# Value products joined with the next unit's scores, more early weight slots, and the gate's denominator sum on GpSimd for 24 steps

## The chip, the cores and the metric

The kernel runs on one core of one Trainium2 chip. The metric is the time of one execution in device microseconds; the runs shown of the kernel before took 986.03 to 987.42 us, with a median of 987.19 us. A separate execution was recorded by the profiler; everything said of single instructions comes from it. The engines are named as the profile names them: PE (TensorE's matmuls), PEld (its weight loads), DVE (VectorE), ACT (ScalarE), POOL (GpSimd), SP (SyncE, which issues the DMAs here).

## The reference

Sliding-window attention is followed by a feed-forward layer whose activation is a rational function.

```python
# q, k, v: (8, 8, 576, 64)
scores = q @ k.T / sqrt(64);  mask: 0 <= pos_q - pos_k < 64
attn = exp(scores - max);  attn = attn / (sum(attn) + 1e-9)
x = (attn @ v)  ->  (4608, 512)
h = x @ w_in                                  # w_in (512, 2048)
P = a[0] + a[1]*h + a[2]*h*h + a[3]*h*h*h
Q = 1 + |b[0]|*|h| + |b[1]|*h*h
g = P / (Q + 1e-6)
out = g @ w_out                               # w_out (2048, 512)
```

All inputs and the output are float32. The kernel keeps the two large products near float32 accuracy by splitting x, g and both weights into a high part (fp32r) and a low part and adding three products: low x high, high x high, high x low.

## The kernel before

**Tiling.** The 4608 tokens are cut into 12 chunks of 384. For each chunk the attention is computed in four *units*, one for each pair of heads, and the feed-forward layer in 16 *steps*, one for each 128 columns of the hidden layer. A unit is: score products (24 small matmuls into the PSUM tile `ps_s`, each on a 64x64 corner of the array), mask and maximum on DVE, exponentials with their sums on ACT, the division on DVE, six transposes on PE back into `ps_s`, a copy to `pT` on ACT, value products (24 matmuls of 128 rows by 64 columns into `ps_x`), and the split of the result into `xh` (ACT) and `xl` (DVE). A step is `ffn1` (12 matmuls of 384 columns into one of two `h` banks, then the gate) and, three steps later, `ffn2` (9 matmuls of 512 columns that add into the three `o` banks).

**The gate.** ACT makes u = h*h, r = |b0 h| and num = a3 h + a2. DVE adds u = |b1| u + r, the sum under the fraction without its constant. ACT takes the logarithm of u + 1.000001 and the exponential of its negative, which is the reciprocal r. DVE then makes the numerator in two operations on `num` (these read h from PSUM), and in four more, all on SBUF, the high part `gh`, and the low part `gl` with one correction. `r`, `u` and `num` have two buffers each, `gh` and `gl` four.

**Weights.** The 32 weight tiles (16 of w_in, 16 of w_out, 512 KB each) are fetched into three slots (`w_st`) and split by `load_weight`: a cast on ACT (`top`), a bit merge on DVE (`w_c`), a cast to the high part on ACT, a subtraction on DVE for the low part. A slot's next fetch is issued once its tile has been split. The first eight of each kind are loaded during the first eight steps, the others during the steps after them, so chunks 0 and 1 run their first eight steps, then chunk 1 and chunk 0 their last eight. Steps 0 to 23 are thus the ones beside which weights are split. The second half of the weights lives in tiles that share memory with the early q, k and v tiles (`early`) of chunk 0.

**What sets the order.** The kernel is recorded, not issued: each call on `pl` becomes an operation with a cost, and `plan` puts the operations of each engine in order by a small model of ready times, due order and costs. `group` makes several matmuls one piece that nothing is put between. Unit work of chunk c is recorded in the steps of the chunk that runs before it, at places given by `OFF` and `AHEAD`. In gaps of PE before the first `o` product, `fill` puts matmuls on a constant tile (`warm`). All instructions that are recorded carry the line of the recorder (L221, and L227 in the changed kernel), so the profile tells them apart by their tiles.

Of the kernel before, what the change touches and what calls it, by code (L numbers as in the profile page):

```python
# [9 lines left out]
F32 = mybir.dt.float32  # L10
# [22 lines left out]
OFF = dict(scores=0, soft=0, norm=0, transpose=1, av=1)  # L33
# [16 lines left out]
class Planner:  # L50
# [27 lines left out]
    @contextmanager  # L78
    def group(self, extra=0):
        g = self.group_op = Op()  # L80
# [24 lines left out]
    def cost(self, engine, method, out, reads, kw, args):  # L105
        if isinstance(out, Late):
            n = out.size // 4
        else:
            n = 1
            for _, k in out.ap[1:]:  # L110
                n *= k
        if engine == "SP":
            parts = 128 if isinstance(out, Late) else (out.ap[0][1] if out.tensor.__class__.__name__ != "DRamTensorHandle" else 0)
            size = mybir.dt.size(out.dtype) * n * (parts or out.ap[0][1])
            return 400, 400, size
        if engine == "PE":
            if method == "transpose":
                return 109, 270, 0
            if isinstance(args[2], Late):
                n = args[2].size // 4  # L120
            else:
                n = 1
                for _, k in args[2].ap[1:]:
                    n *= k
                if args[2].dtype == F32:
                    return (54, 270, 0) if args[1].ap[0][1] == 64 else (58, 225, 0)
            return n * 0.452, n * 0.452 + 165, 0
        if engine == "ACT":
            if "accum_out" in kw:
                return 343, 450, 0  # L130
            f = args[2] if len(args) > 2 else None
            occ = 58 + 0.813 * n
            if n == 512:
                occ = 640 if method == "copy" and getattr(out, "dtype", None) == F16 else 510
            for k in ("scale", "bias"):
                if isinstance(kw.get(k), bass.AP):
                    occ += 92
            if f in (AF.Ln, AF.Exp):
                occ += 55
            return occ, occ + 120, 0  # L140
        if engine == "DVE":
            if method == "tensor_reduce":
                n = 1
                for _, k in reads[0].ap[1:]:
                    n *= k
            if n < 16:
                return 90, 185, 0
            occ = 65 + 1.045 * n
            if isinstance(kw.get("scalar"), bass.AP):
                occ += 62  # L150
            return occ, occ + 85, 0
        if engine == "POOL":
            return (n * 2.0 + 60, n * 2.0 + 100, 0) if method == "tensor_scalar" else (n * 2.4 + 130, n * 2.4 + 170, 0)
# [24 lines left out]
    def plan(self):  # L178
# [6 lines left out]
        for _ in self.ops:  # L185
# [7 lines left out]
            if engine == "SP":  # L193
                dma_free = max(dma_free, start + 1500) + op.dma / 390
                op.end = dma_free + 150
# [47 lines left out]
def swa_rational_ffn(ctx: ExitStack, tc: tile.TileContext, qk, v, w_in, w_out, ab, out):  # L243
# [89 lines left out]
    UNIT = QK + TC * P  # L333
    qk_ring = Ring(ring, 2, [P, QK], F32, "qk")
# [12 lines left out]
    shares = {early[k].tensor.name: f"late_{n}" for k, n in enumerate(("wo_l", "wo_h"))}  # L347
# [7 lines left out]
    def fetch():  # L355
        if not fetch_order:
            return
        which, i = key = fetch_order.pop(0)
        staged[key] = w_ring()
        pl.sync.dma_start(out=staged[key].bitcast(U16)[:, 1:2049], in_=(w_in if which == "in" else w_out)[i])  # L360

    def load_weight(which, i):
# [10 lines left out]
        fetch()  # L373
# [6 lines left out]
    def load_qk(c, hp):  # L380
        qk_t = early[hp // 2][:, hp % 2 * UNIT:hp % 2 * UNIT + QK] if c == 0 else qk_ring()
# [3 lines left out]
        u["k"] = qk_t[:, CH:QK]  # L385

    def load_v(c, hp):
        vt = early[hp // 2][:, hp % 2 * UNIT + QK:hp % 2 * UNIT + UNIT] if c == 0 else vt_ring()
        live[c, hp]["vt"] = vt = vt.rearrange("p (t s) -> p t s", s=P)
        pl.sync.dma_start(out=vt, in_=v[hp, :, c * TC:(c + 1) * TC, :])  # L390
# [15 lines left out]
    def unit_scores(c, hp):  # L406
# [10 lines left out]
        with pl.group(340):  # L417
            for p in range(PR):
                for z in range(2):
                    for e in range(2):  # L420
                        j = 2 * p + e
                        pl.tensor.matmul(ps[z][e * 64:e * 64 + 64, p * P:(p + 1) * P], u["q"][z * 64:z * 64 + 64, j, :],
                                         u["k"][z * 64:z * 64 + 64, j * WIN:j * WIN + P], start=not on_pe, stop=not on_pe or p == PR - 1)
        sm, nmx = u["sm"], u["nmx"] = sm_ring(), small["nmx"]().rearrange("p (z r) -> p z r", z=2)
# [44 lines left out]
    def unit_av(c, hp):  # L469
        u = live.pop((c, hp))  # L470
        ps = ps_x[:, 0:TC * WIN].rearrange("p (t s) -> p t s", s=WIN)
        with pl.group(135):
            for j in range(TC):
                for z in range(2):
                    pl.tensor.matmul(ps[z * 64:z * 64 + 64, j, :], u["vt"][:, j, z * 64:z * 64 + 64],
                                     u["pT"][:, z, j * WIN:(j + 1) * WIN], start=True, stop=True)
        x = ps_x[:, 0:CH]
        xh, xl = (x_sb[x_slot(c)][part][hp] for part in range(2))
        pl.scalar.copy(out=xh, in_=x)
        pl.vector.tensor_tensor(out=xl, in0=x, in1=xh.bitcast(F32), op=ALU.subtract)  # L480

    gs = {}

    def ffn1(c, i):
        h = h_ring()[:, 0:CH]
        n = 0
        for cc in range(NCC):
            with pl.group():
                for w, x in (("wi_h", 1), ("wi_h", 0), ("wi_l", 0)):
                    pl.tensor.matmul(h, weight_piece(w, i, cc), x_sb[x_slot(c)][x][cc], start=n == 0, stop=n == 3 * NCC - 1)  # L490
                    n += 1
# [5 lines left out]
        pl.vector.scalar_tensor_tensor(out=u, in0=u, scalar=b_sb[:, 1:2], in1=r, op0=ALU.mult, op1=ALU.add)  # L497
# [66 lines left out]
    s, seen = 0, {0}  # L564
    for c, i0, i1 in phases:
        if c not in seen:
            seen.add(c)
            for k in range(HP):
                p = C1AT[k] if c == 1 else s - prev + prev // HP * k - AHEAD
                at(p, unit_load, c, k)  # L570
                for n, fn in (("scores", unit_scores), ("soft", unit_soft), ("norm", unit_norm), ("transpose", unit_transpose), ("av", unit_av)):
                    at(max(p + OFF[n], s - prev) if n == "av" else p + OFF[n], fn, c, k)
        prev = i1 - i0
        s += prev

    for load in (load_qk, 0), (load_qk, 1), fetch, (load_v, 0), (load_qk, 2), (load_v, 1), (load_qk, 3), fetch, (load_v, 2), (load_v, 3), None, fetch:
        if load is None:
            pl.sync.dma_start(out=ab_sb, in_=bass.AP(ab.tensor, 0, [[0, P], [1, 6]]))
        elif load is fetch:
            fetch()  # L580
        else:
            load[0](0, load[1])
# [6 lines left out]
    pl.scalar.activation(b_sb, b_raw, AF.Abs)  # L589
# [54 lines left out]
```

## Time and profile before

| | |
|---|---|
| median of the runs shown | 987.19 us |
| the profiled execution | 985.98 us |
| its span, first to last instruction | 984.2 us |
| PE busy | 959.3 us (97%) |
| DVE busy | 914.5 us (93%) |
| ACT busy | 693.1 us (70%) |
| POOL busy | 4.3 us, 20 instructions, all at the start |
| granted PE clock | 0.995 |

A row of a group or of the timeline names engine, operation, and then out<-in by the names of tiles, with the partitions and columns of each. In the timeline the first number is the start from the span's beginning, the second the duration; "x24" means that many records in a row, and a bracket behind a row tells how long the engine had stood still and what released it. Durations of neighbouring rows on one engine overlap by some 0.05 to 0.2 us, so what an instruction takes of its engine is read from start to start.

### The profile page before, as it was taken

What the parts mean: (1) busy time and instruction counts of PE and PEld (TensorE: products, weight loads), DVE (VectorE), ACT (ScalarE), POOL (GpSimd) and SP (SyncE); (2) the same over time, 40 slices, a digit from 0 to 9 for tenths busy, and PEclk for the clock granted to TensorE, in tenths of its full rate; (3) what the DMA queues carried; (4) which work ended last, traced back from release to release, by engine and by line L of the source; (5) the groups of instructions that cost most, each with busy time, mean ns of one, the idle gap of its engine ahead of it and who ended that gap; (6) DMA issues with size and microseconds to landing.
All of it is one profiled execution on the core that took longest, in us unless ns stands there. A gap on an engine that the chain in (4) does not pass through costs nothing.

```text
span 984.2 us, 17685 instructions
## 1 busy us (share of the span) xinstructions
PE 959.3 (97%) x6679; PEld 827.2 (84%) x6679; DVE 914.5 (93%) x1746; ACT 693.1 (70%) x1737; POOL 4.3 (0%) x20
## 2 busy tenths in 40 slices
PE   7798999999999999999999999999999999999998
PEld 4577788888888888888888888888888888888996
DVE  6899999899999999999999999999999999999997
ACT  6888877776667667666767677667666776766664
POOL 1000000000000000000000000000000000000000
PEclk9999999999999999999999999999999999999999
DMA  6654440313103103103102101210310310200000
GB/s 241 213 179 149 140 149 30 108 46 129 39 1 117 51 1 117 35 17 118 34 17 101 51 17 46 88 34 8 113 48 1 117 39 12 100 1 1 33 1 32
DMA packets 24708, 68.24 MB, mean 69 GB/s; under 512 B 2864, under 2 KB 2864, under 8 KB 24624
## 3 DMA queue, kind: packets, MB, share of 16 engines
q1 hardware_dynamic: 24624, 67.12, 20.3%
q8 instruction: 52, 0.85, 0.3%
q14 instruction: 32, 0.26, 0.1%
HBM read 56.89 MB, written 10.22 MB: 68 GB/s over the span
## 4 chain that ended last, share of the span: by engine, by line
PE 75%; DVE 15%; ACT 4%; DMA 3%; issue 1%; SPq 0%; DVEq 0%; ACTq 0%
PE h L221 34%; PE o L221 32%; PE ps_s L221 6%; DVE u L221 5%; DVE num L221 3%; PE ps_x L221 3%; DVE gh L221 2%; ACT sm L221 2%; DVE gl L221 1%; DMA w_st<-w_out 1%; DMA w_st<-w_in 1%; ACT r L221 1%; DVE w_c L221 1%; ACT top L221 1%; DVE wo_l L221 1%
## 5 line engine op out<-in xcount | busy, mean ns | idle before, releaser
L221 PE MATMUL h<-xl,wi_h 128*128 128x384 f32 x768 | 274.2, 357 | 6.0 <-DVE num L221 3.9
L221 PE MATMUL h<-xh,wi_h 128*128 128x384 f32 x768 | 260.1, 339 | 0.0
L221 PE MATMUL h<-xh,wi_l 128*128 128x384 f32 x768 | 259.5, 338 | 0.0
L221 PE MATMUL o<-wo_h,gl 128*128 128x512 f32 x576 | 227.9, 396 | 4.5 <-DVE gl L221 3.3
L221 PE MATMUL o<-wo_l,gh 128*128 128x512 f32 x576 | 228.3, 396 | 0.0
L221 PE MATMUL o<-wo_h,gh 128*128 128x512 f32 x576 | 227.2, 394 | 0.0
L221 ACT ACTIVATE u<-h 128x384 f32<-128x384 f32 x192 | 94.4, 491 | 181.7 <-PE h L221 149.2
L221 PEld LDWEIGHTS h<-xl,wi_h 128*128 128x128 f32 x768 | 144.5, 188 | 43.2 <-issue 6.9
L221 PEld LDWEIGHTS h<-xh,wi_h 128*128 128x128 f32 x768 | 145.0, 189 | 22.4
L221 DVE SCALAR_TENSOR_TENSOR gh<-num,ab_sb,r 128x384 fp32r<-128x384 f32 x192 | 118.2, 615 | 28.5 <-ACT r L221 19.4
L221 PEld LDWEIGHTS h<-xh,wi_l 128*128 128x128 f32 x768 | 144.4, 188 | 0.0
L221 ACT ACTIVATE r<-u 128x384 f32<-128x384 f32 x192 | 101.3, 528 | 55.9 <-DVE u L221 51.3
L221 ACT ACTIVATE num<-h,ab_sb 128x384 f32<-128x384 f32 x192 | 130.0, 677 | 5.9 <-PE h L221 3.7
L221 PEld LDWEIGHTS o<-wo_h,gh 128*128 128x128 f32 x576 | 108.1, 188 | 24.4
L221 DVE SCALAR_TENSOR_TENSOR u<-u,b_sb,r 128x384 f32<-128x384 f32 x192 | 117.9, 614 | 7.1 <-ACT r L221 5.1
L221 DVE SCALAR_TENSOR_TENSOR u<-num,ab_sb,u 128x384 f32<-128x384 f32 x192 | 118.2, 616 | 2.5
L221 DVE SCALAR_TENSOR_TENSOR num<-num,ab_sb,h 128x384 f32<-128x384 f32 x192 | 117.1, 610 | 3.1
L221 PEld LDWEIGHTS o<-wo_h,gl 128*128 128x128 f32 x576 | 108.1, 188 | 11.4 <-DVE gl L221 5.3
L221 ACT ACTIVATE r<-h,ab_sb 128x384 f32<-128x384 f32 x192 | 110.9, 578 | 1.1 <-DVE num L221 1.1
L221 DVE SCALAR_TENSOR_TENSOR u<-u,gh 128x384 f32<-128x384 f32 x192 | 106.5, 554 | 3.7
L221 PEld LDWEIGHTS o<-wo_l,gh 128*128 128x128 f32 x576 | 108.3, 188 | 1.2 <-DVE gh L221 0.3
L221 DVE TENSOR_TENSOR gl<-u,r 128x384 fp32r<-128x384 f32 x192 | 106.0, 552 | 0.4
(69 smaller groups left out, 985.6 us busy)
## 6 DMA issues: line engine op xcount, KB each, us to landing
qk<-qk SPq DMA_DIRECT2D x44, 416.0 KB, 3.4
vt<-v SPq DMA_DIRECT2D x44, 384.0 KB, 4.1
out<-ob SPq DMA_DIRECT2D x33, 256.0 KB, 2.1
w_st<-w_in SPq DMA_DIRECT2D x16, 512.0 KB, 4.2
w_st<-w_out SPq DMA_DIRECT2D x16, 512.0 KB, 4.2
early<-qk SPq DMA_DIRECT2D x4, 416.0 KB, 5.7
early<-v SPq DMA_DIRECT2D x4, 384.0 KB, 8.7
part<-ob SPq DMA_DIRECT2D x3, 256.0 KB, 4.5
```

What stands on the lines that cost most here:

```text
L221: call(*[value(x) for x in args], **{k: value(x) for k, x in kw.items()})
```

## The change

Three things are changed, and the planner's numbers with them.

1. From chunk 3 on, the value products of one unit and the score products of the next unit are recorded as one piece on PE (`av_and_scores`). To that end the value products are moved to the place of the next unit, four steps later than before. `ffn1`'s twelve matmuls become one piece too, for all steps but the first two of chunks 0 and 1.
2. Six more slots for early weights are cut out of the memory of the second half of w_in (`spare`), so that nine weight tiles are fetched at the start without waiting for a slot. The order of the first fetches is a list of its own (`LOADS`). The six numbers a and b no longer have a DMA of their own: they ride behind each q and k tile, and DVE copies them out of the first one.
3. In the first 24 steps the sum u = |b1| u + r is made by two GpSimd instructions, a product with a scalar and an addition, in place of one on DVE.

The planner's costs change for the small matmuls, for value and score products, and for the DMAs.

```diff
+JOIN = 4
+ASIDE = 24
+LOADS = "q0 q1 w0 v0 q2 v1 q3 w1 v2 v3 w2 w3 w4 w5 w6 w7 w8"
...
+    spare = [late.tile([P, H * NCC * P], F32, name=f"early_{n}", tag=f"late_{n}") for n in ("wi_h", "wi_l")]
+    spare_slots = [t[:, k * 1026:(k + 1) * 1026] for k in range(H * NCC * P // 1026) for t in spare]
...
-        staged[key] = w_ring()
+        staged[key] = spare_slots.pop(0) if spare_slots else w_ring()
...
-        fetch()
+        if w.tensor.name.startswith("w_st"):
+            fetch()
...
+    def av_and_scores(c, hp, c2, hp2):
+        with pl.group(-203):
+            value_products(c, hp)
+            score_products(c2, hp2)
+        value_parts(c, hp)
+        score_maximum(c2, hp2)
...
+        whole = ExitStack()
+        if c > 1 or i >= 2:
+            whole.enter_context(pl.group())
...
-        pl.vector.scalar_tensor_tensor(out=u, in0=u, scalar=b_sb[:, 1:2], in1=r, op0=ALU.mult, op1=ALU.add)
+        if steps.index((c, i)) < ASIDE:
+            pl.gpsimd.tensor_scalar(out=u, in0=u, scalar1=b_sb[:, 1:2], scalar2=None, op0=ALU.mult)
+            pl.gpsimd.tensor_tensor(out=u, in0=u, in1=r, op=ALU.add)
+        else:
+            pl.vector.scalar_tensor_tensor(out=u, in0=u, scalar=b_sb[:, 1:2], in1=r, op0=ALU.mult, op1=ALU.add)
...
+    for n, (p, c, k, free) in enumerate(places):
+        joined = n >= HP + JOIN
+        if joined:
+            p = max(p, places[n - 1][3])
+        at(p, unit_load, c, k)
+        if joined:
+            at(p, av_and_scores, *places[n - 1][1:3], c, k)
+        else:
+            at(p, unit_scores, c, k)
+        at(p, unit_soft, c, k)
+        at(p, unit_norm, c, k)
+        at(p + 1, unit_transpose, c, k)
+        if n + 1 < HP + JOIN or n + 1 == len(places):
+            at(max(p + 1, free), unit_av, c, k)
...
+    pl.vector.tensor_copy(out=ab_sb, in_=live[0, 0]["ab"])
+    pl.scalar.activation(b_sb, b_raw, AF.Abs)
```

How the instructions move is seen in three places. The first is PE in the steps in which chunk 3's units are computed: value products go into `ps_x`, score products into `ps_s` from a q and k tile (x12 counts the recorded calls). Before:

```order
L221 MATMUL o_73<-wo_h_1123,gh_186 128x512
L221 MATMUL ps_x<-pT_171,vt_162 64x64 x12
L221 MATMUL h_76<-xl_155,wi_h_134 128x384
L221 MATMUL h_76<-xh_151,wi_h_134 128x384
L221 MATMUL h_76<-xh_151,wi_l_135 128x384
L221 MATMUL ps_s<-qk_161 64x128 x12
L221 MATMUL h_76<-xl_156,wi_h_134 128x384
```

With the change:

```order
L227 MATMUL h_76<-xh_153,wi_h_134 128x384
L227 MATMUL h_76<-xh_153,wi_l_135 128x384
L227 MATMUL ps_x<-pT_173,vt_162 64x64 x12
L227 MATMUL ps_s<-qk_161 64x128 x12
L227 MATMUL o_72<-wo_h_1084,gl_192 128x512
L227 MATMUL o_72<-wo_l_1108,gh_188 128x512
```

The products stood apart with other matmuls between and around them; now they are neighbours between a whole `h` block and an `o` piece. Over the program 37 value products have score products right behind them, where before it were 2.

The second place is DVE in step 4, in the stretch in which weights are split (`w_c`, `wo_l`). Before:

```order
L221 SCALAR_TENSOR_TENSOR num_182<-num_182,ab_sb,h_75 128x384
L221 SCALAR_TENSOR_TENSOR u_181<-u_181,b_sb,r_179 128x384
L221 SCALAR_TENSOR_TENSOR gh_184<-num_182,ab_sb,r_178 128x384
L221 TENSOR_TENSOR wo_l_137<-w_c_168,wo_h_136 128x512
L221 SCALAR_TENSOR_TENSOR u_180<-u_180,gh_184 128x384
L221 TENSOR_TENSOR num_183<-num_183,h_76 128x384
L221 SCALAR_TENSOR_TENSOR u_180<-num_182,ab_sb,u_180 128x384
```

With the change, on DVE and on POOL:

```order
L227 SCALAR_TENSOR_TENSOR gh_186<-num_184,ab_sb,r_180 128x384
L227 SCALAR_TENSOR_TENSOR w_c_170<-w_st_165,top_139 128x512
L227 SCALAR_TENSOR_TENSOR u_182<-u_182,gh_186 128x384
L227 TENSOR_TENSOR num_185<-num_185,h_76 128x384
L227 SCALAR_TENSOR_TENSOR u_182<-num_184,ab_sb,u_182 128x384
```

```order
L227 TENSOR_SCALAR u_182<-u_182,b_sb 128x384
L227 TENSOR_TENSOR u_182<-u_182,r_180 128x384
L227 TENSOR_SCALAR u_183<-u_183,b_sb 128x384
L227 TENSOR_TENSOR u_183<-u_183,r_181 128x384
```

The row with `b_sb` has gone from DVE and stands as two on POOL, 48 in all; DVE's other operations keep their order.

The third place is DVE at the start. Before, behind the first maximum:

```order
L221 TENSOR_REDUCE nmx_172<-ps_s 128x6
L221 SCALAR_TENSOR_TENSOR w_c_167<-w_st_164,top_138 128x512
L221 TENSOR_SCALAR nmx_172<-nmx_172 128x6
L221 TENSOR_REDUCE nmx_173<-h_75 128x3
L221 TENSOR_REDUCE nmx_173<-h_76 128x3
L221 TENSOR_TENSOR wi_l_135<-w_c_167,wi_h_134 128x512
```

With the change:

```order
L227 COPY ab_sb<-early_158 128x6
L227 TENSOR_REDUCE nmx_174<-ps_s 128x6
L227 TENSOR_REDUCE nmx_175<-h_75 128x3
L227 TENSOR_SCALAR nmx_174<-nmx_174 128x6
L227 TENSOR_REDUCE nmx_175<-h_76 128x3
L227 TENSOR_SCALAR nmx_175<-nmx_175 128x6
L227 SCALAR_TENSOR_TENSOR w_c_169<-early_wi_h,top_138 128x512
```

The first weight's merge (`w_c`) has moved behind both maxima and their scaling.

More of the change, by code (lines that the diff above doesn't have):

```diff
@@ L79, in group @@
     def group(self, extra=0):
+        if self.group_op is not None:
+            self.group_op.occ += extra
+            yield
+            return
         g = self.group_op = Op()
@@ L193, in plan @@
             if engine == "SP":
-                dma_free = max(dma_free, start + 1500) + op.dma / 390
-                op.end = dma_free + 150
+                dma_free = max(dma_free, start + 750) + op.dma / (300 if start < 8000 else 390)
+                op.end = dma_free + 1550
             for o in op.after:
@@ L242, in swa_rational_ffn @@
 @with_exitstack
-def swa_rational_ffn(ctx: ExitStack, tc: tile.TileContext, qk, v, w_in, w_out, ab, out):
+def swa_rational_ffn(ctx: ExitStack, tc: tile.TileContext, qk, v, w_in, w_out, out):
     nc = tc.nc
@@ L345, in swa_rational_ffn @@
     ob_ring = Ring(ring, 2, [P, DO], F32, "ob")
-    shares = {early[k].tensor.name: f"late_{n}" for k, n in enumerate(("wo_l", "wo_h"))}
+    shares = {t.tensor.name: f"late_{n}" for t, n in zip(early + spare, ("wo_l", "wo_h", "wi_h", "wi_l"))}
     pl = Planner(nc, dict(DVE=4700, ACT=2100, PE=WARM * 430 + 1200, POOL=5000, SP=750), shares)
@@ L486, in ffn1 @@
         n = 0
[L487 to L491, printed above, removed]
+        whole = ExitStack()
+        if c > 1 or i >= 2:
+            whole.enter_context(pl.group())
+        with whole:
+            for cc in range(NCC):
+                with pl.group():
+                    for w, x in (("wi_h", 1), ("wi_h", 0), ("wi_l", 0)):
+                        pl.tensor.matmul(h, weight_piece(w, i, cc), x_sb[x_slot(c)][x][cc], start=n == 0, stop=n == 3 * NCC - 1)
+                        n += 1
         r, u, num = (tmp[n]() for n in ("r", "u", "num"))
@@ L562, in swa_rational_ffn @@
     fetch_order += [tuple(call[1:]) for s in range(total) for call in todo.get(s, ()) if call[0] is load_weight]
[L564 removed]
+    s, seen, places = 0, {0}, []
     for c, i0, i1 in phases:
@@ L567, in swa_rational_ffn @@
             seen.add(c)
[L568 to L572, printed above, removed]
+            places += [(C1AT[k] if c == 1 else s - prev + prev // HP * k - AHEAD, c, k, s - prev if c > 1 else 0) for k in range(HP)]
         prev = i1 - i0
         s += prev
[L576 to L579, printed above, removed]
+    for n, (p, c, k, free) in enumerate(places):
[12 more added lines that the diff above has]
+            at(max(p + 1, free), unit_av, c, k)
+    for load in LOADS.split():
+        what, k = load[0], int(load[1])
+        if what == "w":
             fetch()
         else:
-            load[0](0, load[1])
+            (load_qk if what == "q" else load_v)(0, k)
+    pl.vector.tensor_copy(out=ab_sb, in_=live[0, 0]["ab"])
+    pl.scalar.activation(b_sb, b_raw, AF.Abs)
     for k in range(HP):
```

42 lines of the change are left out of this document (27 added, 15 removed).

## The prediction

> **What bounds the kernel now.** I read the profiled execution from the outside in: first each engine's busy time by stage, then the operations of the engine that is full in each stage, then the waits. The execution took 985.98 us around a span of 984.2 us; the median of the runs shown is 987.19 us, so 1.2 us are added at the end. In the table by stage the columns are the stretch, its length, then busy time and instructions of PE, PEld, DVE, ACT and POOL, the granted clock, and DMA.
>
> ```profile
> 33.00:165.00 132.00, 120.15 (x795) 99.57 (x795) 130.33 (x254) 107.12 (x251) 0.00 (x0) 0.99 0.42 142
> 165.00:300.00 135.00, 133.14 (x992) 115.06 (x991) 125.54 (x244) 96.50 (x260) 0.00 (x0) 1.00 0.20 65
> 300.00:960.00 660.00, 660.00 (x4530) 579.43 (x4530) 619.79 (x1174) 455.56 (x1133) 0.00 (x0) 1.00 0.15 48
> ```
>
> There are two regimes. From 165 us on PE has no gap worth the name (660.00 of 660 us between 300 and 960), and DVE keeps 6% in hand. From 33 to 165 us, while the weights are still being split, it is the other way round: DVE is busy 130.33 of 132 us, PE stands still for 11.85 us, POOL does nothing. The waits of that stretch (total, times, longest) say for whom PE stands:
>
> ```profile
> PEld h L221 <- DVE num L221: 6.2, 7, 1.7
> PE o L221 <- DVE gl L221: 3.1, 7, 0.8
> PE ps_s L221 <- DMA qk<-qk: 2.7, 1, 2.7
> ```
>
> So a PE saving counts in full after 165 us and hardly before it; a DVE saving counts before 165 us, up to the 11.85 us that PE has to give, and not after. Before 33 us it is a chain of short waits.
>
> **The joined piece.** This is the one term that the trace of before prices directly. Here are a value product of a unit between two matmuls of h, a score product between two matmuls of h, and a place where the old order happened to put the two side by side.
>
> ```profile
> 301.03 0.34 PE L221 MATMUL h<-xh,wi_h 128*128 128x384 f32 x1
> 301.20 0.34 PE L221 MATMUL h<-xh,wi_l 128*128 128x384 f32 x1
> 301.47 0.92 PE L221 MATMUL ps_x<-pT,vt 128*64 128x64 f32 x24
> 302.60 0.34 PE L221 MATMUL h<-xh,wi_h 128*128 128x384 f32 x1
> ...
> 306.97 0.34 PE L221 MATMUL h<-xh,wi_l 128*128 128x384 f32 x1
> 307.24 0.89 PE L221 MATMUL ps_s<-qk 64*64 64x128 f32 x24
> 308.34 0.34 PE L221 MATMUL h<-xh,wi_h 128*128 128x384 f32 x1
> 308.52 0.34 PE L221 MATMUL h<-xh,wi_l 128*128 128x384 f32 x1
> ```
>
> ```profile
> 193.70 0.40 PE L221 MATMUL o<-wo_l,gh 128*128 128x512 f32 x1
> 193.94 0.39 PE L221 MATMUL o<-wo_h,gh 128*128 128x512 f32 x1
> 194.26 0.92 PE L221 MATMUL ps_x<-pT,vt 128*64 128x64 f32 x24
> 195.11 0.89 PE L221 MATMUL ps_s<-qk 64*64 64x128 f32 x24
> 196.21 0.34 PE L221 MATMUL h<-xh,wi_h 128*128 128x384 f32 x1
> ```
>
> Durations overlap, so I count starts. Matmuls of h follow each other after 0.17 to 0.18 us. The value product takes PE from 301.20 to 302.60, 1.40 us, where two such steps would take 0.35: it costs 1.05 us. The score product costs 308.34 - 306.97 - 0.35 = 1.02 us. Together 2.07. Side by side they take 196.21 - 193.94 = 2.27 us, less one step behind an o (0.24) and one of h (0.17): 1.86 us. The joined piece thus saves 0.21 us: what is spent on going from the 128-row, 64-column shape back to the full array and from there into the 64x64 shape. The new order has 37 such neighbours where the old one had 2: 35 x 0.21 = **7.3 us**, all but a few after 165 us, where PE is the bound. It shrinks only if something else fills the gap. DVE has 660 - 619.79 = 40 us to spare there, and the value product comes four steps later than its inputs exist, so it waits for less than before. A unit's transposed scores and its v tile are held four steps longer; both are wanted again a whole unit later. The twelve matmuls of h as one piece can hold others back by 12 x 0.175 = 2.1 us at most; nothing in that regime is due sooner. Bounds: 0 and 7.5 us.
>
> **The start.** Here the chain is visible row by row.
>
> ```profile
> 8.18 0.77 ACT L221 CAST top<-w_st 128x512 f16<-128x512 bf16 x1 [6.16 <-DMA w_st<-w_in]
> 10.23 0.36 ACT L221 ACTIVATE sm<-ps_s,nmx 128x128 f32<-128x128 f32 x1
> 31.82 0.77 ACT L221 CAST top<-w_st 128x512 f16<-128x512 bf16 x1 [2.04 <-DMA w_st<-w_out]
> ```
>
> ```profile
> 8.98 0.69 DVE L221 SCALAR_TENSOR_TENSOR w_c<-w_st,top 128x512 uint32<-128x512 uint32 x1 [1.54 <-ACT top L221]
> 9.59 0.16 DVE L221 TENSOR_SCALAR nmx<-nmx 128x6 f32<-128x6 f32 x1
> ```
>
> The first exponentials (10.23) wait for the scaled maximum, which DVE makes at 9.59 behind the first weight split, which waits for ACT's cast (to 8.95). In the new order maximum and scaling come first, and the exponentials start when the cast ends: 1.28 us earlier, and the rest of chunk 0's attention hangs on them. Up to 31.82 ACT waits 2.04 us for a weight that was only sent for when one of three slots came free, and DVE's split of it waits behind ACT; six slots more remove that. The scores of chunk 1 waited 2.7 us for their q and k (the row of waits above); these stand behind the same loads in both orders, and I count nothing for them. Upper end 1.28 + 2.04 = 3.3 us, lower end 0, since a gap that closes on one engine may open on the next. I take **2.6 us**. The scaled b now stands first on ACT and all of ACT waits behind it for q's first tile; that is free, since ACT waited 6.16 us there anyway. The removed transfer of a and b costs and frees nothing, and the wider q tiles (838 columns for 832) nothing either.
>
> **GpSimd.** What leaves DVE:
>
> ```profile
> 89.94 0.62 DVE L221 SCALAR_TENSOR_TENSOR u<-u,b_sb,r 128x384 f32<-128x384 f32 x1
> 90.47 0.62 DVE L221 SCALAR_TENSOR_TENSOR u<-num,ab_sb,u 128x384 f32<-128x384 f32 x1
> ```
>
> Each takes 0.53 us of DVE's time (start to start; the 0.62 overlaps the next), 24 times: 12.7 us. If nothing else happened, DVE's 132 us became 119 us, below PE's 120, and the gain would be capped by PE's idle time, 11.85 - 2.7 = 9.1 us (the 2.7 are the wait for q and k).
>
> What it may cost: 48 POOL instructions beside a full DVE. Nothing of 384 columns on POOL is in the trace. The nearest rows are its selects of 128 columns at the start, where DVE copies ran beside two of them:
>
> ```profile
> 2.83 0.29 POOL L285 TENSOR_SCALAR_AFFINE_SELECT mask<-mask 64x128 bf16<-64x128 bf16 x1
> 3.85 0.33 POOL L285 TENSOR_SCALAR_AFFINE_SELECT mask<-mask 64x128 bf16<-64x128 bf16 x1
> ```
>
> ```profile
> 3.15 0.27 DVE L290 COPY mask<-mask 64x128 bf16<-64x128 bf16 x1 [2.02 <-POOL mask L285]
> 3.85 0.38 DVE L295 COPY mask<-mask 64x128 bf16<-64x128 bf16 x1
> ```
>
> The same copy took 0.27 us with no select beside it and 0.38 us beside a select that took 0.33 instead of 0.29. So the two engines do hinder each other: DVE lost 0.11 us, a third of the POOL instruction's time. For 384 columns an instruction takes between 0.29 us (all overhead) and 0.87 us (all columns); I take the middle, 0.58, as an estimate. A third of it is 0.19 us, times 48 is 9.3 us lost on DVE. Net 12.7 - 9.3 = **3.4 us** gained. Ends: DVE loses nothing (9.1 us gained), or it stands still for all of a POOL instruction whenever it has an operation with two inputs in SBUF next. How often that is, the groups of DVE operations between 33 and 160 us tell (busy us, mean ns | idle):
>
> ```profile
> L221 DVE SCALAR_TENSOR_TENSOR w_c<-w_st,top 128x512 uint32<-128x512 uint32 x26 | 17.8, 687 | 2.5 <-ACT top L221 2.3
> L221 DVE SCALAR_TENSOR_TENSOR num<-num,ab_sb,h 128x384 f32<-128x384 f32 x24 | 14.6, 608 | 0.0
> L221 DVE SCALAR_TENSOR_TENSOR u<-num,ab_sb,u 128x384 f32<-128x384 f32 x23 | 14.1, 613 | 0.0
> L221 DVE SCALAR_TENSOR_TENSOR gh<-num,ab_sb,r 128x384 fp32r<-128x384 f32 x23 | 14.1, 612 | 0.0
> L221 DVE TENSOR_TENSOR num<-num,h 128x384 f32<-128x384 f32 x24 | 13.1, 547 | 0.0
> L221 DVE SCALAR_TENSOR_TENSOR u<-u,gh 128x384 f32<-128x384 f32 x23 | 12.7, 552 | 0.0
> L221 DVE TENSOR_TENSOR gl<-u,r 128x384 fp32r<-128x384 f32 x22 | 12.1, 551 | 0.0
> L221 DVE TENSOR_TENSOR wo_l<-w_c,wo_h 128x512 fp32r<-128x512 f32 x15 | 10.2, 681 | 0.0
> L221 DVE TENSOR_TENSOR wi_l<-w_c,wi_h 128x512 fp32r<-128x512 f32 x12 | 8.2, 686 | 0.0
> ```
>
> Only the two num rows, 27.7 us, read h from PSUM and so have one input in SBUF; the other seven, 89.2 us, have two. That is 76%, some 70% with the attention's reductions, which read PSUM. Then 48 x 0.87 x 0.7 = 29 us are lost against 12.7 saved: 16.5 us slower.
>
> The Trainium skill, "SBUF — State Buffer", section "Who interferes with whom", states that end as the rule: a DVE instruction with two SBUF inputs and a GpSimd instruction that reads SBUF exclude each other, and whichever comes second waits for the whole of the first. The trace's 0.11 of 0.33 us neither proves nor refutes it, for that copy has one input and may have met only the select's tail. [...]
>
> The new wait: ACT's logarithm now waits for POOL's sum, and behind it on ACT's queue stand the next step's squares and the casts of weights. The chain grows by two POOL instructions less 0.53 us, 0.6 us at the middle estimate; ACT has 132 - 107 = 25 us to spare there and each step has two sets of buffers, so I price it at nothing; without that slack it would be 24 x 0.6 = 15 us.
>
> **The sum.** 985.98 - 7.3 - 2.6 - 3.4 = 972.7 us for an execution like the profiled one, 973.9 with the 1.2: **974 us**.
>
> **Rivals.**
> *POOL costs DVE nothing*: 985.98 - 7.3 - 2.6 - 9.1 + 1.2 = 968 us. For it: the copy's 0.11 us may be a matter of starting beside another instruction, once, and not of every element. Against: two stretched selects and a stretched copy are all the overlaps that there are, and none is free of it.
> *POOL holds DVE.* Slower than before as soon as each of the 48 instructions holds DVE for more than (12.7 + 7.3 + 2.6) / 48 = 0.47 us; at the full end 985.98 - 7.3 - 2.6 + 16.5 + 1.2 = 994 us. For it: 70% of DVE's work there has two SBUF inputs, and DVE has 1.67 us of slack in 132. Against: the measured loss was a third.
> *The joins do not pay*, since the new order puts other waits on PE after 165 us: 974 + 7.3 = 981 us. Against: the side-by-side rows at 194 us, and DVE's 40 us of slack. That the joins are not made at all is excluded by the order.
>
> **How the numbers follow.** Forecast 0.46, POOL free 0.24, joins without gain 0.10, POOL holds DVE 0.20. Of the last, 0.14 lies beyond 0.2% slower, 0.05 within 0.2% (what a measurement of this kernel can tell from no change), 0.01 below. Faster: 0.46 + 0.24 + 0.10 + 0.01 = 0.81; same 0.05; slower 0.14. The range goes from 965 us (POOL free, and the start at its upper end) to 988 us, which leaves out the worse part of the POOL rival and little below.
>
> **What would show it.** In the changed profile: 37 places where the rows of ps_x and ps_s follow each other, and the stretch from 300 to 960 us shorter per chunk by 4 x 0.21 us. First exponential near 9 us, no 2 us wait of ACT near 32 us. POOL's rows of 384 columns near 0.6 us; DVE's two-input rows in the first 24 steps longer than 0.55 to 0.61 us, or gaps before them, by some 9 us in all. PE's idle time between 33 and 165 us down by about 3 us beside the 2.7 for q and k. I am wrong if DVE's rows there stretch by more than 0.47 us per POOL instruction, or if PE shows new gaps after 165 us.

## The result, and the profile after

| | before | changed |
|---|---|---|
| median | 986.61 us | 994.04 us |
| lowest to highest | 986.03 to 987.42 us | 993.19 to 994.62 us |
| span of the profiled execution | 984.2 us | 991.8 us |

The ratio is 1.0074, with an interval of 1.0061 to 1.0087: the kernel became 7.4 us slower, where 974 us were forecast. (986.61 us is the median of six runs; the 987.19 us that the prediction starts from is that of the first three of them.) I read the profile after in the order of the prediction. First the table by stage of the changed kernel (stretch, length, busy time and count of PE, PEld, DVE, ACT, POOL, clock, DMA). Its second row runs from the first step's operation that makes `gl`, the last of the gate, to that of step 23; I use such a window for other kernels too, since it holds the same work in each.

```profile
33.00:165.00 132.00, 113.41 (x686) 93.49 (x687) 125.41 (x213) 102.17 (x234) 58.23 (x46) 0.96 0.36 123
36.50:171.25 134.75, 117.22 (x740) 96.17 (x740) 127.96 (x217) 102.56 (x226) 57.52 (x45) 0.95 0.35 120
165.00:300.00 135.00, 134.39 (x1031) 116.61 (x1031) 126.41 (x244) 95.78 (x250) 0.89 (x1) 0.99 0.20 64
300.00:960.00 660.00, 656.23 (x4529) 578.05 (x4528) 617.25 (x1176) 461.33 (x1144) 0.00 (x0) 1.00 0.15 49
```

Before 165 us PE's idle time rose from 11.85 to 18.59 us, where it should have fallen. After 300 us PE, which had no gap before, has one of 3.77 us, and makes 4529 products where it made 4530: the joins have moved nothing there.

**The start** went the way that was foreseen. Two rows of ACT's timeline:

```profile
7.69 0.77 ACT L227 CAST top<-early_wi_h 128x512 f16<-128x512 bf16 x1 [2.33 <-DMA early_wi_h<-w_in]
8.33 0.35 ACT L227 ACTIVATE sm<-ps_s,nmx 128x128 f32<-128x128 f32 x1
```

The first exponential starts at 8.33 us in place of 10.23. No 2 us wait of ACT is left near 32 us. The first step's `gl` starts at 36.50 us, against 41.00 before: 4.5 us ahead. Not all of this is the change. Single executions differ by some 2 us at the start: in b_beside and b_half below, whose instructions on PE, DVE and ACT stand in the order of the kernel before, the first exponential starts at 9.31 and 9.60 us and the first `gl` at 38.85 and 39.19. What the start is worth is therefore read from the medians of a_noaside and c_nospare.

**The 24 steps beside the weights** lost more than that. The window in the second row above is 134.75 us long; in the kernel before, the same work ran from 41.00 to 164.91 us, 123.91 us. The groups of POOL from 30 to 250 us, which holds nearly all of its work in these steps:

```profile
L227 POOL TENSOR_SCALAR u<-u,b_sb 128x384 f32<-128x384 f32 x24 | 34.2, 1423 | 88.7 <-ACT u L227 88.7
L227 POOL TENSOR_TENSOR u<-u,r 128x384 f32<-128x384 f32 x24 | 27.8, 1158 | 9.5 <-ACT r L227 7.8
```

And the groups of DVE in the same window (busy us, mean ns | idle time before them):

```profile
L227 DVE SCALAR_TENSOR_TENSOR gh<-num,ab_sb,r 128x384 fp32r<-128x384 f32 x23 | 17.8, 775 | 0.1
L227 DVE SCALAR_TENSOR_TENSOR w_c<-w_st,top 128x512 uint32<-128x512 uint32 x24 | 16.4, 685 | 0.0
L227 DVE SCALAR_TENSOR_TENSOR u<-num,ab_sb,u 128x384 f32<-128x384 f32 x23 | 16.4, 714 | 0.1
L227 DVE SCALAR_TENSOR_TENSOR u<-u,gh 128x384 f32<-128x384 f32 x23 | 15.1, 658 | 0.3
L227 DVE TENSOR_TENSOR gl<-u,r 128x384 fp32r<-128x384 f32 x24 | 14.7, 614 | 0.0
L227 DVE SCALAR_TENSOR_TENSOR num<-num,ab_sb,h 128x384 f32<-128x384 f32 x23 | 14.0, 608 | 4.6 <-ACT r L227 4.1
L227 DVE TENSOR_TENSOR num<-num,h 128x384 f32<-128x384 f32 x24 | 13.1, 547 | 1.3 <-ACT u L227 1.0
L227 DVE TENSOR_TENSOR wo_l<-w_c,wo_h 128x512 fp32r<-128x512 f32 x14 | 11.0, 789 | 0.0
...
L227 DVE TENSOR_TENSOR sm<-sm,rs 128x768 f32<-128x768 f32 x5 | 6.4, 1271 | 0.0
```

The two `num` rows, whose second input comes from PSUM, take 608 and 547 ns as before, to the nanosecond. Most rows with two inputs in SBUF have grown: `gh` from 612 to 775 ns, `u<-num` from 613 to 714, `u<-u,gh` from 552 to 658, `gl` from 551 to 614, `wo_l` from 681 to 789, the division `sm` from 951 to 1271. One has not: `w_c`, with 685 ns against 686; b_beside will show why that is no exception. The Trainium skill, "SBUF — State Buffer", section "Who interferes with whom", draws the line at the same place: one SBUF input keeps DVE off the ports that it shares with GpSimd, as long as it is in none of its 2-port modes; two do not. And DVE, which had next to no idle time in these groups, now waits 4.1 us for ACT's `r`.

**The joined pieces** are made as planned. In the timeline of PE, `ps_x` and `ps_s` are neighbours between products of `o`:

```profile
314.95 0.40 PE L227 MATMUL o<-wo_h,gh 128*128 128x512 f32 x1
315.28 0.92 PE L227 MATMUL ps_x<-pT,vt 128*64 128x64 f32 x24
316.13 0.89 PE L227 MATMUL ps_s<-qk 64*64 64x128 f32 x24
316.94 0.50 PE L227 MATMUL o<-wo_h,gl 128*128 128x512 f32 x1
317.28 0.40 PE L227 MATMUL o<-wo_l,gh 128*128 128x512 f32 x1
```

Products of `o` follow each other after 0.235 us, so the pair costs 317.28 - 314.95 - 2 x 0.235 = 1.86 us, the very number that the prediction read at 194 us of the trace before.

### The profile page after: what moved, and what is told of

It reads as the page before. It is cut to its first block, busy times and chain, and to the rows that moved or that the text cites. A ratio compares the mean times of both kernels' runs of the same rounds, so it can differ in the third digit from the quotient of the medians.

```text
span 991.8 us, 17777 instructions
## 1 busy us (share of the span) xinstructions
PE 958.4 (97%) x6671; PEld 829.4 (84%) x6674; DVE 917.2 (92%) x1723; ACT 699.9 (71%) x1737; POOL 66.3 (7%) x68
## 4 chain that ended last, share of the span: by engine, by line
PE 70%; DVE 13%; ACT 10%; issue 3%; POOL 1%; DMA 0%; ACTq 0%; DVEq 0%; SPq 0%
PE o L227 31%; PE h L227 31%; PE ps_s L227 6%; DVE u L227 4%; ACT sm L227 4%; PE ps_x L227 3%; ACT r L227 2%; DVE num L227 2%; DVE gh L227 2%; DVE sm L227 1%; ACT u L227 1%; POOL u L227 1%; ACT num L227 1%; DVE gl L227 1%; DVE nmx L227 1%
## 5 line engine op out<-in xcount | busy, mean ns | idle before, releaser
L227 PE MATMUL h<-xl,wi_h 128*128 128x384 f32 x768 | 261.7, 341 | 4.8 <-DVE num L227 3.9
L227 PE MATMUL o<-wo_h,gl 128*128 128x512 f32 x576 | 237.8, 413 | 12.3 <-DVE gl L227 9.5
L227 DVE SCALAR_TENSOR_TENSOR gh<-num,ab_sb,r 128x384 fp32r<-128x384 f32 x192 | 121.6, 633 | 8.8 <-PE h L227 2.2
L227 DVE SCALAR_TENSOR_TENSOR u<-num,ab_sb,u 128x384 f32<-128x384 f32 x192 | 120.3, 627 | 2.8
L227 DVE SCALAR_TENSOR_TENSOR u<-u,gh 128x384 f32<-128x384 f32 x192 | 108.8, 566 | 3.1
L227 DVE TENSOR_TENSOR num<-num,h 128x384 f32<-128x384 f32 x192 | 104.9, 548 | 3.3 <-ACT u L227 1.0
```

Of the source, the lines that this page charges most:

```text
L227: call(*[value(x) for x in args], **{k: value(x) for k, x in kw.items()})
```

## The experiments

The first four experiments ask which of the three parts costs the time, and how: does POOL hold DVE's instructions up, does the longer gate make others wait, or does the new order of the matmuls eat what the joins give?

### a_noaside: the change without GpSimd

```diff
-ASIDE = 24
+ASIDE = 0
```

> The changed kernel with the gate's sum of all steps on DVE again; joins, slots and planner costs as changed. Theory A (GpSimd's two instructions hold DVE for as much as they take off it, and lengthen the gate, so that the loss of some 7 us that stands at 200 us comes from them): the loss before 200 us goes, 985 to 988 us. Theory B (the loss comes from the new order, above all from the undivided block of twelve matmuls): little changes, 992 to 996 us.

Measured: 981.53 us, 0.9957 of before (0.9942 to 0.9972), below both of the ranges that were expected. The change as a whole took 994.04, so the GpSimd sum costs 12.5 us (11.8 if each is held against the runs of the kernel before that were made beside it, 986.61 and 985.92). But the other two parts give only 4.4 us, not the 9.9 that the prediction's terms for them add up to. The same 24 steps as above, by the same two events, in this kernel:

```profile
36.57:159.74 123.17, 112.94 (x738) 94.38 (x731) 121.98 (x239) 101.75 (x227) 0.00 (x0) 1.00 0.40 132
```

With GpSimd they take 134.75 - 123.17 = 11.6 us more. DVE is busy 127.96 us instead of 121.98, although 23 of its operations at 0.53 us, 12.2 us, have gone: it lost 6.0 + 12.2 = 18.2 us to 45 POOL instructions, **0.40 us for each**. And it is idle 6.79 us instead of 1.19: the other **5.6 us** are gaps. The granted clock differs too, 0.95 in the changed kernel's window and 1.00 in this one, but it is not what makes most of the difference: best_aside below loses 12.4 us in the same window at 0.98, and the window of b_half, at 1.00, is 5.3 us longer than that of the kernel before.

### b_aside: before, and the GpSimd sum alone

```diff
-        pl.vector.scalar_tensor_tensor(out=u, in0=u, scalar=b_sb[:, 1:2], in1=r, ...)
+        if steps.index((c, i)) < 24:
+            pl.gpsimd.tensor_scalar(out=u, in0=u, scalar1=b_sb[:, 1:2], scalar2=None, op0=ALU.mult)
+            pl.gpsimd.tensor_tensor(out=u, in0=u, in1=r, op=ALU.add)
+        else: ...
```

> The kernel before with nothing changed but the gate's sum of the first 24 steps on GpSimd. Theory A: DVE loses about 0.3 us for each of the 48 instructions, 14 to 15 us against 12.7 us saved, and the gate gets longer: 2 to 9 us slower than before (989 to 996 us). Theory B: GpSimd is not at fault, and the kernel is as fast as before or faster by up to 9 us (978 to 987 us).

Measured: 995.77 us, 1.0100 of before (1.0085 to 1.0116), 9.9 us slower. The 24 steps of before, and of this kernel:

```profile
41.00:164.91 123.91, 114.77 (x757) 95.19 (x756) 122.37 (x239) 99.56 (x231) 0.00 (x0) 1.00 0.38 127
```

```profile
41.65:173.18 131.53, 115.57 (x747) 95.93 (x745) 125.16 (x216) 100.84 (x235) 58.36 (x44) 0.97 0.37 119
```

DVE is busy 2.8 us longer with 12.2 us less to do: 15.0 us lost, 0.34 us for each of 44 POOL instructions; its gaps grow from 1.54 to 6.37 us, by 4.8. Here is who waits along the chain of the gate in that window (total, times, longest):

```profile
PEld o L221 <- DVE gl L221: 14.8, 10, 2.9
ACT r L221 <- POOL u L221: 14.7, 13, 2.0
PE o L221 <- DVE gl L221: 13.1, 11, 2.6
```

ACT waits for POOL's sum before it can take the logarithm, and PE's products of `o` then wait for `gl`; in the kernel before they did so for 3.1 us. So the sum is slower in the old order as well, and both causes are there: DVE held up, and a chain that the prediction priced at nothing.

### a_nojoin: the change without the joined pieces

```diff
-JOIN = 4
+JOIN = 100
```

> The changed kernel with value products and score products recorded apart again, in their places of before; all else as changed. If the joins save their 7.3 us after all: 1001 us. If what they save on PE is lost again because the transposes now find the divided tile late (0.23 us a unit, seen between 300 and 960 us of the changed kernel): 993 to 996 us, and the transposes' wait is gone.

Measured: 996.60 us, 1.0111 (1.0094 to 1.0128). The joins are thus worth 2.6 us within the change, not 7.3. But the transposes' wait is not gone, as the table below tells: in seven chunks it is 3.0 us longer than in the kernel before (9.37 against 6.38), although nothing is joined, and the seven chunks take 3.07 us longer. So about half of the added wait is there with the blocks of twelve and the planner's new costs alone, without the joins. The sections on c_nowhole and c_late take this up.

### b_beside: GpSimd work that nothing waits for

The kernel before in its own order on PE, DVE, ACT and SP, with two POOL instructions per step on `gh` and `gl` whose results nobody reads. DVE keeps its own sum. What changes is only that POOL is at work beside it.

```diff
+        if steps.index((c, i)) < 24:
+            pl.gpsimd.tensor_scalar(out=idle, in0=gh.bitcast(F32), scalar1=b_sb[:, 1:2], ...)
+            pl.gpsimd.tensor_tensor(out=idle, in0=gh.bitcast(F32), in1=gl.bitcast(F32), op=ALU.add)
```

> The kernel before, in which GpSimd does work beside it in the first 24 steps whose result nobody reads: for each step a product of gh with a scalar and a sum of gh and gl, 384 columns, written to a tile of its own. DVE keeps all of its work. Theory A (the two engines hold each other): DVE's two-input rows grow as in the changed kernel and the run is slower by what DVE loses, 10 to 16 us (997 to 1003 us). If only the longer gate of the changed kernel cost time: as before, 987 us.

Measured: 999.24 us, 1.0135 (1.0120 to 1.0150), 13.3 us slower with nothing waiting for it. Its 24 steps:

```profile
38.85:178.35 139.50, 119.83 (x755) 97.14 (x756) 137.42 (x240) 102.16 (x231) 72.90 (x46) 0.98 0.35 116
```

DVE's gaps are 2.1 us, as good as before; it is busy 137.42 - 122.37 = 15.05 us longer for the same operations: 0.33 us for each of the 46 POOL instructions in the window, much as in b_aside. Which operations pay shows in the groups of DVE from 33 to 175 us:

```profile
L221 DVE SCALAR_TENSOR_TENSOR w_c<-w_st,top 128x512 uint32<-128x512 uint32 x24 | 21.4, 894 | 0.6 <-ACT top L221 0.6
...
L221 DVE SCALAR_TENSOR_TENSOR gh<-num,ab_sb,r 128x384 fp32r<-128x384 f32 x24 | 14.8, 618 | 0.0
L221 DVE SCALAR_TENSOR_TENSOR num<-num,ab_sb,h 128x384 f32<-128x384 f32 x24 | 14.4, 601 | 0.0
...
L221 DVE TENSOR_TENSOR sm<-sm,rs 128x768 f32<-128x768 f32 x5 | 7.0, 1393 | 0.0
...
L221 DVE TENSOR_SCALAR sums<-sums 128x6 f32<-128x6 f32 x5 | 1.8, 357 | 0.0
```

`w_c`, which now happens to stand where POOL starts, went from 687 to 894 ns; `gh`, which was the worst hit in the changed kernel, is back at 618. So among operations with two inputs in SBUF it is not the operation but its place beside POOL's that decides. Even an operation of six columns (`sums`) takes 357 ns where it took 167. It reads one tile and a constant, so two inputs are not the whole rule; whether it ran in one of the 2-port modes no run here shows. One meeting in detail, from the timelines of POOL and of DVE:

```profile
114.04 1.02 POOL L221 TENSOR_TENSOR idle<-gh,gl 128x384 bf16<-128x384 f32 x1 [1.36 <-DVE gl L221]
116.31 1.85 POOL L221 TENSOR_SCALAR idle<-gh,b_sb 128x384 bf16<-128x384 f32 x1 [1.25 <-DVE gh L221]
```

```profile
113.82 0.60 DVE L221 SCALAR_TENSOR_TENSOR num<-num,ab_sb,h 128x384 f32<-128x384 f32 x1
114.34 1.27 DVE L221 TENSOR_TENSOR wi_l<-w_c,wi_h 128x512 fp32r<-128x512 f32 x1
```

`wi_l` takes 0.69 us alone. Here it takes 1.27 and ends 0.55 us after POOL's instruction (115.06): it got little or nothing done while POOL was at work. The other way round, POOL's next one takes 1.85 us, where the shortest of its kind takes 1.24. The skill's section named above says that whichever comes second blocks; these rows agree.

The next four ask where the joins' gain went, and what the slots are worth.

### c_nowhole: a_noaside, and the twelve matmuls of h no longer one piece

```diff
-        if c > 1 or i >= 2:
+        if False:
             whole.enter_context(pl.group())
```

> The changed kernel without GpSimd's part (981.5 us) and with the twelve matmuls of a step recorded in four pieces of three again. If the undivided block is what makes the transposes stand and wait for their input (0.23 us a unit): the wait goes, the stretch from 300 to 960 us gets the joins' 0.2 us a unit, and the time is 974 to 976 us. If the block is not at fault: 981 to 983 us.

Measured: 977.79 us, 0.9922 (0.9905 to 0.9938): 3.7 us less than a_noaside, between the two ranges.

### c_late: a_noaside, and the planner told that the division ends later

Only the order changes: the planner now takes the division's result to be there 0.8 us later, and puts the transposes that wait for it further back.

```diff
-            return occ, occ + 85, 0
+            return occ, occ + 85 + (800 if n == 768 and method == "tensor_tensor" else 0), 0
```

> The changed kernel without GpSimd's part (981.5 us), in which the planner is told that the division of the scores is ready 0.8 us later, so that it puts about three more matmuls ahead of each unit's transposes. If PE's new waits are these transposes standing too early on the queue: 975 to 977 us, and the wait ahead of them is gone. If the work itself is late (DVE or ACT fuller than before), the wait only moves: 981 to 983 us.

Measured: 978.16 us, 0.9926 (0.9909 to 0.9943): 3.4 us less than a_noaside, between the two ranges again.

### c_late_nowhole: both

> Both of the two edits together. If either alone takes the wait away, this is like the better of them, 974 to 977 us; if the gain is not in the transposes' place at all, 981 to 983 us.

Measured: **973.38 us**, 0.9876 (0.9859 to 0.9893), just below the expected 974 to 977. This is faster than both kernels, and 4.4 us faster than the better of the two single edits, so neither of them alone had done all.

The three are read together. From each trace I took the start of the first product of `o` in step 56 and in step 168, seven chunks apart, and, for the 28 units in between, the time from the start of the last matmul ahead of a unit's transposes to the start of the first transpose, added up. Without a wait that is 0.17 us behind an `h` and 0.23 behind an `o`, 5 to 6.5 us for 28. The column of step 56 is not to be compared between kernels with and without blocks of twelve, since with them the first product of `o` stands behind the whole `h` block: a_noaside is 2.3 us ahead of the kernel before in it, but 3.7 us by the first products of `h` of step 187. The difference of two steps in one kernel is free of this.

```text
kernel           step 56   step 168   seven chunks   ahead of 28 first transposes
before           336.07    883.20     547.12          6.38
changed          345.27    893.05     547.78         12.38
a_noaside        333.78    880.93     547.15         11.88
a_nojoin         345.70    895.88     550.19          9.37
c_nowhole        331.85    875.88     544.03          7.09
c_late           333.28    877.07     543.79          6.28
c_late_nowhole   330.10    871.25     541.14          5.32
```

In c_late_nowhole seven chunks take 5.98 us less than before, over 28 joins 0.21 us each: what the prediction had priced. In a_noaside they take as long as before, and its transposes stand 5.5 us longer: that is where the gain went. How it comes about is seen in a_noaside's timelines of DVE and of PE:

```profile
449.84 0.17 DVE L227 TENSOR_SCALAR sums<-sums 128x6 f32<-128x6 f32 x1 [1.21 <-ACT sm L227]
450.05 0.19 DVE L227 RECIPROCAL rs<-sums 128x6 f32<-128x6 f32 x1
450.27 0.96 DVE L227 TENSOR_TENSOR sm<-sm,rs 128x768 f32<-128x768 f32 x1
```

```profile
450.37 0.34 PE L227 MATMUL h<-xh,wi_l 128*128 128x384 f32 x1
451.38 0.85 PE L227 MATMUL ps_s<-ident,sm 128*128 128x128 f32 x6 [0.68 <-ACT ob L227]
451.98 0.48 PE L227 MATMUL o<-wo_h,gl 128*128 128x512 f32 x1
```

DVE waits for ACT's exponentials, divides until 451.23, and the transposes start 0.15 us later, 1.01 us after the matmul ahead of them. (The row names ACT's `ob`; the division's end fits to 0.15 us, here and elsewhere.) Between 300 and 960 us, 26 of 30 first transposes in a_noaside start within 0.16 us of the division's end, 7 in the kernel before, none in c_late_nowhole, where the timelines of DVE and PE have 0.8 us in between:

```profile
408.09 0.95 DVE L227 TENSOR_TENSOR sm<-sm,rs 128x768 f32<-128x768 f32 x1
```

```profile
409.67 0.34 PE L227 MATMUL h<-xh,wi_l 128*128 128x384 f32 x1
409.85 0.82 PE L227 MATMUL ps_s<-ident,sm 128*128 128x128 f32 x6
```

The groups of PE between 300 and 960 us say the same as idle time (after the bar), for a_noaside and for c_late_nowhole:

```profile
L227 PE MATMUL ps_s<-ident,sm 128*128 128x128 f32 x180 | 25.3, 277 | 3.2 <-ACT ob L227 2.0 <-DVE sm L227 1.1
```

```profile
L227 PE MATMUL ps_s<-ident,sm 128*128 128x128 f32 x180 | 24.5, 272 | 0.0
```

Moving the transposes alone (c_late) removes that wait, but leaves one of 1.8 us on products of `o`, so blocks of twelve cost something elsewhere. The group of c_late in the same stretch:

```profile
L227 PE MATMUL o<-wo_h,gl 128*128 128x512 f32 x416 | 170.1, 409 | 1.8 <-ACT ob L227 1.8
```

Breaking up the blocks alone (c_nowhole) leaves 1.8 us of the transposes' wait (7.09 against 5.32). The two edits act on different things, as DVE shows. Its wait for ACT's exponentials ahead of the scaling of the sums, between 300 and 960 us, is 22.0 us in a_noaside and in the changed kernel (30 times each), 19.4 us in c_late and 13.9 us in a_nojoin, which all have the blocks. It is 2.3 us in c_late_nowhole and in no row of the waits of c_nowhole and of the kernel before, which have none. So it is with the blocks that the division comes late; c_late leaves it late and only moves the transposes out of its way. Why the exponentials come later beside the blocks is open.

Only both free PE for good, as the table by stage of c_late_nowhole shows: 660.00 of 660 us, with 4560 products in them against 4530 before.

```profile
300.00:960.00 660.00, 660.00 (x4560) 587.41 (x4557) 627.22 (x1185) 459.04 (x1140) 0.00 (x0) 1.00 0.15 47
```

### c_nospare: a_noaside without the six slots

```diff
-LOADS = "q0 q1 w0 v0 q2 v1 q3 w1 v2 v3 w2 w3 w4 w5 w6 w7 w8"
+LOADS = "q0 q1 w0 v0 q2 v1 q3 w1 v2 v3 w2"
...
-    spare_slots = [t[:, k * 1026:(k + 1) * 1026] ...]
+    spare_slots = []
```

> The changed kernel without GpSimd's part (981.5 us) and without the six early slots: three slots and three early weights as in the kernel before; a and b still ride behind q and k. The start was priced at 2.6 us (0 to 3.3), of which 2.04 came from the slots: 983 to 984 us. If the gain of 4.4 us at the first step is all the slots': 985 to 986 us. If the start's gain is lost before 165 us, since DVE is the bound there: 981 to 982 us.

Measured: 986.12 us, 1.0007 of before (0.9997 to 1.0017). Against a_noaside that is 4.6 us by the medians and 3.4 us by the profiled spans (983.2 and 979.8). All that a_noaside gains over the kernel before hangs on the slots. Here are ACT's waits for tiles of w_in from 5 to 60 us, of c_nospare and of a_noaside:

```profile
ACT top L227 <- DMA w_st<-w_in: 3.7, 3, 2.3
```

```profile
ACT top L227 <- DMA early_wi_h<-w_in: 2.3, 1, 2.3
```

The 2.3 us are the wait for the very first weight, the same in both; the missing slots add only waits of 0.5 and 0.9 us there. More tells how many weights ACT has cast by 60 us: 15 in a_noaside, 11 in c_nospare, 13 in the kernel before. The first `gl` of c_nospare is still early (36.99 us, against 41.00 before), but 4.0 us ahead there are down to 1.0 at step 7 (86.90 against 87.87), where a_noaside is 5.9 us ahead (81.93). So a start ahead of weights that are not there yet is lost again.

The last two ask for the price of the GpSimd sum in the best order, and how it goes with the length of its instructions.

### best_aside: c_late_nowhole with the GpSimd sum

```diff
-ASIDE = 0
+ASIDE = 24
```

> The kernel of 973.4 us (late division, step in four pieces, no GpSimd) with GpSimd's part of the change put back. If GpSimd's price is a matter of the two engines and not of one order of the instructions: slower by the 10 to 13 us that the two other pairs showed, 983 to 987 us. If it was an accident of the changed kernel's order: 970 to 977 us.

Measured: 986.53 us, 1.0004 of before (0.9994 to 1.0013): 13.2 us more than c_late_nowhole. In three orders of the kernel the sum on GpSimd thus costs 9.9, 12.5 and 13.2 us; held against the runs of the kernel before made beside each, 9.9, 11.8 and 12.8. The 24 steps of best_aside, and of c_late_nowhole:

```profile
35.79:171.85 136.06, 115.69 (x750) 95.23 (x749) 127.06 (x217) 101.10 (x228) 64.12 (x45) 0.98 0.35 118
```

```profile
37.25:160.91 123.66, 113.36 (x737) 94.54 (x730) 122.45 (x238) 99.76 (x226) 0.00 (x0) 1.00 0.40 132
```

By the working of a_noaside, DVE lost 4.6 + 12.2 = 16.8 us, 0.37 us for each of 45 POOL instructions, and its gaps grew by 7.8 us.

### b_half: b_beside on half the columns

```diff
-            pl.gpsimd.tensor_scalar(out=idle, in0=gh.bitcast(F32), ...)
+            pl.gpsimd.tensor_scalar(out=idle[:, 0:CH // 2], in0=gh.bitcast(F32)[:, 0:CH // 2], ...)
```

(and the addition in the same way)

> The kernel before with GpSimd's unread work beside it, on 192 columns in place of 384 (the 384 columns took 13.3 us). If DVE is held for as long as GpSimd streams its data: half of it and a little more, 992 to 994 us. If each GpSimd instruction costs DVE a fixed stretch: 998 to 1000 us.

Measured: 990.59 us, 1.0045 (1.0029 to 1.0062): 4.6 us slower, a third of b_beside's 13.3, and below both of the ranges that were expected. The profiled execution was the fastest of its four, with 988.62 us. Its 24 steps:

```profile
39.19:168.37 129.18, 116.23 (x762) 95.60 (x761) 127.89 (x240) 100.81 (x231) 52.76 (x46) 1.00 0.38 125
```

DVE is busy 5.5 us longer than before, 0.12 us per POOL instruction instead of 0.33. What POOL's instructions take when nothing hinders them is in the views of one tile, as shortest, median and longest duration in ns. For b_beside:

```profile
L221 POOL TENSOR_SCALAR idle<-gh,b_sb x24: 1242/1856/3135, 36.2 to 175.9; 128x384 bf16<-128x384 f32 x24
L221 POOL TENSOR_TENSOR idle<-gh,gl x24: 1006/1019/2339, 39.5 to 179.0; 128x384 bf16<-128x384 f32 x24
```

and for b_half:

```profile
L221 POOL TENSOR_SCALAR idle<-gh,b_sb x24: 763/1376/2581, 36.5 to 165.5; 128x192 bf16<-128x192 f32 x24
L221 POOL TENSOR_TENSOR idle<-gh,gl x24: 594/604/1914, 39.9 to 169.1; 128x192 bf16<-128x192 f32 x24
```

The shortest fall to about 0.6 of their time with half the columns, DVE's loss to 0.37 of its own. A fixed price per instruction would have left it at 0.33 us, a price in proportion to the columns at 0.17; it came out below both. A fixed price per instruction is thus excluded; the law is not settled by one run.

## Why the prediction was wrong, point by point

**The GpSimd term**, with 3.4 us gained, is the step that failed. It costs 9.9 to 13.2 us. Three things in it were off.

- *The length of an instruction.* I took 0.58 us, the middle between the ends of 0.29 and 0.87 that I drew from selects of 128 columns. Both ends were too low: undisturbed, the product takes 1.24 us and the sum 1.00. Scaling with the columns was not the error alone, for the selects were another operation.
- *The hold on DVE.* A third of 0.58 us, 0.19 for each, was to make 9.3 us. The third came from a single pair of copies, and the one taken as free had a memset of POOL beside it (at 3.18 us, 0.20 us long). Measured: 0.33 us (b_beside) to 0.40 us (in the change), 15 to 18.2 us in windows of 44 to 46 instructions, against 12.2 saved there. This alone turns the sign. The full hold of my upper end, 29 us, did not come: part of the time POOL is the one that waits, with instructions of up to 2.5 us in the changed kernel. That this is the whole reason why the price stays at 0.33 us is argued from these rows, not shown.
- *The wait priced at nothing.* Two instructions at 1.42 and 1.16 us less 0.53 make the gate's chain 2.05 us longer, not 0.6. I let two sets of buffers and ACT's 25 us of slack carry it; without them I had named 24 x 0.6 = 15 us. In the three orders it costs DVE 4.8, 5.6 and 7.8 us of gaps, since DVE's next numerator waits for ACT, and ACT for POOL; in b_beside, where nothing waits for POOL, the gaps grow by only 0.5 us.

The rival "POOL holds DVE" was the right mechanism, and the time it gave for its full end, 994 us, is the measured one, but that is luck, for it came by other terms: DVE lost less than its 29 us, the chain and the missing gain of the joins made up for that. Its threshold of 0.47 us per instruction was wrong for that reason: the hold was 0.33 to 0.40, below it, and the kernel was slower all the same. With what the runs showed, the point from which the change loses is, as an estimate, (12.7 + 4.4 - 5.6) / 48 = 0.24 us.

**The joined piece.** The 0.21 us of one join is right, in the changed kernel's own rows and in c_late_nowhole's seven chunks. That it would reach the end was not. The step that failed is the sentence that the twelve matmuls of `h` as one piece hold back nothing that is due sooner: in every kernel with these blocks DVE waits 14 to 22 us for the exponentials ahead of the division, and the planner's order put the transposes right behind the division, at the head of PE's queue, where they stood for 5.5 us of the 5.98 that the joins had given. Without the joins, in a_nojoin, 3.0 us of this wait are there already. So the rival "the joins do not pay" held as well, through the mechanism it named (other waits on PE after 165 us); I gave it 0.10 and only on its own, never together with the other. DVE's 40 us of slack, which I set against it, did not help: an engine with idle time on average can still finish one operation too late. Which of the planner's changed costs has a part in the transposes' place I have not separated.

**The start** was right in kind and undersized: 2.6 us predicted, with an upper end of 3.3; a_noaside's seven chunks take as long as before, so that its 4.4 us (2.8 to 5.7 by its interval) are the start's, up to small differences in the last steps, and without the slots they are gone. The slots do more than remove the one wait of 2.04 us that I counted, since the weights of the next steps come earlier too (15 cast by 60 us, against 13 before).

**The sum, redone.** Start -4.4, joins -5.98 and, by the waits, about as much back (both in seven chunks), GpSimd +11.6 in the 24 steps: 986.6 - 4.4 + 11.6 = 993.8 against 994.0 measured. (The 12.5 us between the medians are no term of their own here, being the change less a_noaside.) Without GpSimd and with an order that lets the joins through, the parts give 986.6 - 4.4 - 5.98 x 37/28 = 974.3; c_late_nowhole took 973.4. The lower end of the range, 965 us, does not follow from its own terms: POOL free gives 968, and the start at its upper end takes 0.7 off that.

**The signs named beforehand.** First exponential near 9 us: 8.33, right in kind. No 2 us wait near 32 us: right. 37 neighbours of `ps_x` and `ps_s`: right. Each chunk after 300 us shorter by 0.84 us: wrong in the change, right in c_late_nowhole. POOL's rows near 0.6 us: wrong by a factor of two. DVE's operations longer by some 9 us: 15 to 18. PE's idle time before 165 us down: wrong. Of the two signs that were to prove me wrong, new gaps on PE after 165 us came; the stretch of more than 0.47 us did not.

## What to carry to other kernels

Before work is moved from a full DVE to GpSimd, run the same GpSimd instructions beside the old kernel with results that nobody reads: what that costs (13.3 us here) is to be held against what DVE is spared (12.7 us), and the chain that the instruction joins is to be priced at its new full length, not at the slack of the engine behind it. A saving on a full engine arrives only if nothing else is put at the head of its queue too early; so beside the durations, look at how far ahead of each use its input is ready, before and after. Where the planner puts a use right behind its input, as the transposes behind the division here, 0.8 us more of latency, in its table alone, were worth 3.4 us.

## What the runs showed that was not expected

- On POOL the product with a scalar (one tile input) takes longer than the sum of two tiles: 1.24 against 1.00 us for 384 columns, undisturbed. Between 192 and 384 columns that is 2.5 and 2.1 ns a column.
- POOL is held up too: the product's median rose from 1.25 us in the changed kernel to 1.86 us in b_beside, with 3.1 us the longest.
- DVE operations of six columns are caught too: 167 to 357 ns for the scaling of the sums in b_beside.
- POOL work that nothing depends on, 73 us in a stretch of 139, made the whole kernel 1.35% slower.
